# Top-k attention and an MLP mixer on one core: where the dummy values lie, how many thresholds are negated, and what lengths the planner counts with

## The chip, the cores and the metric

One NeuronCore of a Trainium2 chip runs the whole kernel in one launch. The metric is the device time in microseconds (us) of that core. Engines are named as the profile names them: PE is TensorE's matmul (PEld its weight load), DVE is VectorE, ACT is ScalarE, POOL is GpSimd, SP is SyncE, which here only issues DMAs.

## The reference

For each of 8 batches and 8 heads, with 576 rows of 64 numbers, it computes top-k attention, and then an MLP mixer over the concatenated heads:

```
scores = scale * q @ k.T                       # 576 x 576 for each head
kth    = the 32nd largest of each row          # top_k = 32
attn   = softmax(where(scores >= kth, scores, -1e9))
x      = concat over heads (attn @ v)          # 8 x 576 x 512
h  = relu(x.T @ w_tok1) @ w_tok2;  u = x + h.T
h2 = relu(u @ w_ch1) @ w_ch2;      out = u + h2
```

## The kernel before

The 64 heads are worked in 32 pairs of two. A pair has nine score tiles of 128 rows by 576 columns: four units of two tiles each (one tile for each head) and one unit of one tile, which holds the last 64 rows of both heads. There are 160 units and 288 tiles.

One unit goes through this chain. PE makes the scores into PSUM tiles called big (L363, or L354 for the small unit). ACT copies them to S in SBUF (L417). For each tile DVE takes the top 8 of each of seven segments of the row into cd (L424) and then, with two rounds of MAX8 and MATCH_REPLACE8 and a last MAX8 (L427, L428, L435), an upper threshold thi: an element that is surely in the top 32, at a rank of about 24. ACT takes Sign of S against thi (L438) into sg and sums it into cnt, which tells how many elements lie above thi. POOL multiplies S by sg into X (L441), so that the elements already counted are turned over and the others stay. Beside the 576 products of a tile, X has twelve more columns: DVE writes dummy values into nine of them (L449), large positive or large negative ones by cnt, so that the eighth largest value of the products and the dummies together is just the 32nd largest of the row. DVE's MAX8 over 587 columns finds it: tlo (L453).

With tlo known, a unit takes one of three forms, chosen by the pair and the unit (`FORMS = ("DRDRD", "ADADA")`, pairs in turn). Form D: ACT makes E = exp(S) (L461), DVE negates the unit's thresholds into nt (L463), and POOL makes Z = (S + nt) * 16, clamps it to a mask M and multiplies E by M into Pm (L466, L469, L472). Form R: ACT makes a penalty M (L479), PE makes the scores again and adds the penalty (L500), and ACT takes exp into Pm (L505). Form A: ACT takes exp into a PSUM tile (L510), and DVE compares and multiplies into Pm (L513). A DMA transposes Pm into PT; when the five units of a pair are there, PE multiplies PT by the values (L386) and DVE divides (L401, L402). After every fourth pair the mixer of that batch runs on PE and ACT (L552 to L626), in between the next pairs' work.

No order of this is written out by hand. Each step is added to a planner with an engine, an expected length, a due time and its dependences (`plan.add("DVE", 0.1, due, ...)`). The planner plays the engines forward: on each engine it takes the step that can start first, and among steps that can start at the same moment (within 0.03) the one that is due first. The due times are multiples of T, the planned time for a tile, from the table W. A step on another engine is taken to see a result HOP after its end. Buffers are taken by the planner too: six S, two X, two sg, three Pm, four big. The instructions are then issued in the planned order, and each engine works through its own in that order; the waits between engines are set from what each instruction reads and writes.

The product is written by one instruction for a whole unit. In a unit of two tiles its output is two rows of 576, 588 apart, and the twelve columns of the first tile lie between the two rows:

```
XW = S + 12
out=X.t[:, 0:n, 0:S]                  # L442, the product of n tiles
out=X.t[:, h, S:XW]...[:, :, 0:3]     # L450, the dummy values of tile h
out=nt.t[:, 0:n]                      # L464, the negated thresholds of n tiles
```

The planner lets the dummy values depend on the tile's own Sign alone (`[cts[h]]`, L452). In the built program, the first L449 of a unit waits for POOL, and so for the product.

Of the kernel before, what the change touches and what calls it, by code (L numbers as in the profile page):

```python
# [8 lines left out]
P = 128  # L9
# [5 lines left out]
LOW = float(2.0**20)  # L15
# [11 lines left out]
BIG = float(2.0**60)  # L27
# [18 lines left out]
class Plan:  # L46
# [3 lines left out]
    HOP = 0.07  # L50
# [120 lines left out]
def kernel(  # L171
# [11 lines left out]
    nc = tc.nc  # L183
    f32 = mybir.dt.float32
# [3 lines left out]
    ALU = mybir.AluOpType  # L188
# [20 lines left out]
    def sbt(name, shape, dt):  # L209
        return sb.tile(shape, dt, name=name, tag=name)  # L210
# [22 lines left out]
    tlo = sbt("tlo", [P, NT + 7], f32)  # L233
# [41 lines left out]
    for t in Xs:  # L275
        nc.vector.memset(t[:, :, S:XW], -BIG)
# [14 lines left out]
    def pair_ops(p):  # L291
# [115 lines left out]
        nm = plan.add("DVE", 0.95, tv + T, norm, [o], acq=[rd], use=[O, X])  # L407
# [4 lines left out]
    def unit_ops(i0, n, s, S_, om, p, g, scores, qkT):  # L412
# [28 lines left out]
        xm = plan.add("POOL", 0.06 + 1.22 * n, te + W["xm"] * T, lambda: nc.gpsimd.tensor_tensor(  # L441
            out=X.t[:, 0:n, 0:S], in0=S_.t[:, 0:n, :], in1=sg.t[:, 0:n, :], op=ALU.mult),  # L442
# [16 lines left out]
        if form == "D":  # L459
            E, M, Z, nt = Buf("E"), Buf("M"), Buf("Z"), Buf("nt")  # L460
            ex = plan.add("ACT", 0.14 + 0.43 * n, te + W["ex"] * T, lambda: nc.scalar.activation(  # L461
                out=E.t[:, 0:n, :], in_=S_.t[:, 0:n, :], func=AF.Exp, scale=scale / UP), evs, acq=[E], use=[S_])
# [9 lines left out]
            last = [plan.add("POOL", 0.06 + 1.22 * n, te + W["pm"] * T, lambda: nc.gpsimd.tensor_tensor(  # L472
                out=Pm.t[:, 0:n, 0:S], in0=E.t[:, 0:n, :], in1=M.t[:, 0:n, :], op=ALU.mult),
                [mk, ex], acq=[Pm], use=[E, M])]
        elif form in ("R", "Q"):
# [7 lines left out]
            else:  # L483
                nt, Z = Buf("nt"), Buf("Z")
                tn = plan.add("DVE", 0.08, te + W["tn"] * T, lambda: nc.vector.tensor_scalar(
                    out=nt.t[:, 0:n], in0=tlo[:, r0 - n + 1 : r0 + 1], scalar1=-(1.0 - 2.0**-24), scalar2=None,
                    op0=ALU.mult), ms, acq=[nt])
                zs = [plan.add("POOL", 0.76, te + W["z"] * T + 0.01 * h, lambda h=h: nc.gpsimd.tensor_scalar(
# [3 lines left out]
                ws = [plan.add("POOL", 0.06 + 0.55 * n, te + W["mk"] * T, lambda: nc.gpsimd.tensor_scalar(  # L492
# [378 lines left out]
```

## Time and profile before

| | us |
|---|---|
| median of 3 runs | 1008.28 (1005.54 to 1013.48) |
| the profiled execution | 1007.34 |
| its span, from the first to the last instruction | 1005.5 |
| mean granted clock of TensorE over the span | 0.839 of full speed |
| busy in the span: PE, DVE, ACT, POOL | 840.6, 830.2, 758.1, 707.6 |

The durations that the rows below give come from the profiled execution. Busy time of an engine is the union of its instructions' times; neighbouring instructions on DVE overlap, so the sum over groups is larger than the engine's busy time. A row of a group gives busy time in us and the mean of one instruction in ns, then the idle time of the engine just before these instructions and what ended it. Most of the work runs evenly from about 20 us to 940 us; the last 35 us are the last batch's mixer on PE and ACT.

### The profile page before, as it was taken

Reading aid. Unit: us, or ns where it says so; the run is one execution under the profiler, and the core shown is the slowest. Engines: PE = TensorE matmul, PEld = TensorE weight load, DVE = VectorE, ACT = ScalarE, POOL = GpSimd, SP = SyncE. Lnnn points to the kernel's source line nnn. Section 1 sums busy time; section 2 is a strip of 40 time slices with the busy share of each in tenths; the row PEclk is TensorE's granted clock in tenths of the full one; section 3 lists DMA queues with packets and bytes.
Section 4 is the critical chain, followed back from the end, with each engine's and each line's share of the span. In section 5 each row is a group of like instructions: output and inputs, shape, how many; then the busy total and the mean of one; then the engine's idle time right before and its main releaser. Section 6 shows DMA issues by size and latency. Waiting matters only on the chain.

```text
span 1005.5 us, 19071 instructions
## 1 busy us (share of the span) xinstructions
PE 840.6 (84%) x5318; PEld 475.5 (47%) x5318; DVE 830.2 (83%) x4868; ACT 758.1 (75%) x1415; POOL 707.6 (70%) x478
## 2 busy tenths in 40 slices
PE   6767679897888979989789978789889897889776
PEld 3434445454454544545445544445445454454443
DVE  4888888888888998889898967999988899988820
ACT  5776768887698877889788776888878797888531
POOL 2878876786786778678776767778777787777600
PEclk9575669996699977899599975999879896899878
DMA  6595724346243553535354452445626364332311
GB/s 134 92 166 97 138 61 83 78 88 143 49 93 70 121 117 52 107 70 139 64 93 95 87 112 45 90 95 98 126 55 98 65 142 82 61 58 60 78 30 51
DMA packets 313011, 90.04 MB, mean 90 GB/s; under 512 B 305728, under 2 KB 307648, under 8 KB 312896
## 3 DMA queue, kind: packets, MB, share of 16 engines
q1 hardware_dynamic: 308944, 84.68, 42.2%
q0 software_dynamic: 2752, 3.77, 2.6%
q8 instruction: 43, 0.70, 0.3%
q14 instruction: 72, 0.59, 0.2%
q10 hardware_dynamic: 1200, 0.30, 0.1%
HBM read 35.85 MB, written 9.44 MB: 45 GB/s over the span
## 4 chain that ended last, share of the span: by engine, by line
POOL 34%; DVE 26%; PE 25%; ACT 8%; issue 4%; DMA 2%; SPq 0%; POOLq 0%; ACTq 0%; DVEq 0%
POOL X L441 14%; POOL Pm L472 9%; DVE cd L424 8%; DVE tlo L453 6%; POOL Z L466 6%; PE big L386 6%; PE big L363 5%; PE big L613 5%; PE big L595 5%; POOL M L469 4%; ACT sg L438 3%; DVE cd L428 3%; DVE X L449 2%; DVE nt L463 2%; DVE Pm L513 1%
## 5 line engine op out<-in xcount | busy, mean ns | idle before, releaser
L441 POOL TENSOR_TENSOR X<-S,sg 128x1152 f32<-128x1152 f32 (+1 forms) x160 | 344.1, 2156 | 146.4 <-ACT sg L438 141.2
L424 DVE MAX8 cd<-S 128x8 f32<-128x82 f32 (+1 forms) x2016 | 398.8, 230 | 12.9 <-ACT S L417 12.4
L363 PE MATMUL big<-kT,qT 64*128 64x64 f32 (+1 forms) x1296 | 300.3, 524 | 61.5 <-DVE Pm L513 16.5
L438 ACT ACTIVATE sg<-S,thi 128x576 bf16<-128x576 f32 x288 | 223.1, 775 | 120.6 <-DVE thi L435 112.1
L363 PEld LDWEIGHTS big<-kT,qT 64*128 64x128 f32 x1296 | 160.7, 223 | 199.5 <-issue 90.7
L453 DVE MAX8 tlo<-X 128x8 f32<-128x587 f32 x288 | 219.1, 761 | 0.1
L417 ACT COPY S<-big 128x576 f32<-128x576 f32 x288 | 171.8, 635 | 34.1 <-PE big L363 29.6
L472 POOL TENSOR_TENSOR Pm<-E,M 128x1152 bf16<-128x1152 bf16 (+1 forms) x79 | 169.4, 2145 | 7.0 <-DMA PT<-Pm 0.6
L386 PE MATMUL big<-vb,PT 128*128 128x65 bf16 (+1 forms) x1600 | 138.0, 216 | 34.9 <-DMA PT<-Pm 28.4
L466 POOL TENSOR_SCALAR Z<-S,nt 128x576 f32<-128x576 f32 x142 | 105.7, 745 | 83.6 <-DVE nt L463 71.0
L386 PEld LDWEIGHTS <-PT 128*128 128x128 bf16 (+1 forms) x1600 | 97.2, 106 | 76.6 <-DMA PT<-Pm 30.1
L595 PE MATMUL big<-UT,wc1b 128*128 128x512 bf16 (+1 forms) x768 | 110.7, 299 | 16.3 <-ACT S L417 5.7
L449 DVE TENSOR_SCALAR X<-kdum,cnt 128x9 f32<-128x9 f32 x288 | 53.2, 211 | 84.2 <-POOL X L441 82.5
L613 PE MATMUL big<-wc2b,H 128*128 128x512 bf16 (+1 forms) x480 | 114.8, 383 | 3.1 <-ACT S L417 1.9
L427 DVE MAX8 m<-cd 128x8 f32<-128x14 f32 x576 | 97.2, 170 | 0.1
L428 DVE MATCH_REPLACE8 cd<-m,cd 128x14 f32<-128x14 f32 x576 | 97.2, 169 | 0.0
L595 PEld LDWEIGHTS <-wc1b 128*128 128x128 bf16 x768 | 55.3, 101 | 70.6 <-issue 26.5
L469 POOL TENSOR_SCALAR M<-Z 128x1152 bf16<-128x1152 f32 (+1 forms) x79 | 82.9, 1049 | 6.6
L461 ACT ACTIVATE E<-S 128x1152 bf16<-128x1152 f32 (+1 forms) x79 | 84.2, 1066 | 1.8
L513 DVE SCALAR_TENSOR_TENSOR Pm<-S,tlo,big 128x576 bf16<-128x576 f32 x78 | 62.5, 804 | 10.6 <-ACT big L510 9.8
L601 ACT ACTIVATE H<-big 128x576 bf16<-128x576 f32 x96 | 59.5, 648 | 14.2 <-PE big L595 13.9
L613 PEld LDWEIGHTS <-H 128*128 128x128 bf16 (+1 forms) x480 | 44.5, 101 | 50.0 <-issue 4.8
(74 smaller groups left out, 852.0 us busy)
## 6 DMA issues: line engine op xcount, KB each, us to landing
qL<-in_q_dram SPq DMA_DIRECT2D x64, 128.0 KB, 2.8
vL<-in_v_dram SPq DMA_DIRECT2D x64, 128.0 KB, 2.8
out_dram<-ob SPq DMA_DIRECT2D x16, 512.0 KB, 3.3
kL<-in_k_dram SPq DMA_DIRECT2D x62, 128.0 KB, 2.8
PT<-Pm SPq DMA_TRANSPOSE x160, 3.4
wc1b<-in_moe_w_ch_dram POOLq DMA_DIRECT2D x4, 384.0 KB, 5.2
wc2b<-in_moe_w_ch_dram POOLq DMA_DIRECT2D x4, 384.0 KB, 5.4
qL<-in_q_dram SPq DMA_DIRECT2D x64, 16.0 KB, 2.3
```

The source lines that it names most:

```text
L363: nc.tensor.matmul(out=flat(bs[h].t)[:, lo:hi], lhsT=qT.t[r, g * P : (g + 1) * P], rhs=kT.t[r, lo:hi], start=True, stop=stop,)
L386: nc.tensor.matmul(out=o[:, g, :], lhsT=src[0:kr, (5 * h if g < 4 else 0) + j, :], rhs=vb.t[0:kr, j, h, :], start=(j == 0), stop=(j == 4),)
L417: evs = [plan.add("ACT", 0.54, t + W["ev"] * T + W["evh"] * h * T, lambda h=h: nc.scalar.copy(out=S_.t[:, h, :], in_=flat(s[h].t)[:, 0:S]) ...
L424: segs = [plan.add("DVE", 0.146, th + W["seg"] * T + 0.01 * a, lambda a=a, cd=cd, h=h: nc.vector.max(cd.t[:, a, :], S_.t[:, h, bounds[a] : ...
L428: c_ = lambda n_, cd=cd, m8=m8: (lambda: nc.vector.match_replace(cd.t[:, :, 0:n_], m8.t[:, :], cd.t[:, :, 0:n_], NEG))
L438: cts.append(plan.add("ACT", 0.77, th + W["ct"] * T, lambda h=h, i=i, r=r: nc.scalar.activation(out=sg.t[:, h, :], in_=S_.t[:, h, :], func ...
L441: xm = plan.add("POOL", 0.06 + 1.22 * n, te + W["xm"] * T, lambda: nc.gpsimd.tensor_tensor(out=X.t[:, 0:n, 0:S], in0=S_.t[:, 0:n, :], in1= ...
L453: m = plan.add("DVE", 0.69, te + W["m5"] * T + 0.3 * h * T, lambda h=h, r=r: nc.vector.max(tlo[:, r : r + 8], X.t[:, h, 0 : XW - 1]), [dm, ...
L466: zs = [plan.add("POOL", 0.76, te + W["z"] * T + 0.01 * h, lambda h=h: nc.gpsimd.tensor_scalar(out=Z.t[:, h, :], in0=S_.t[:, h, :], scalar ...
L472: last = [plan.add("POOL", 0.06 + 1.22 * n, te + W["pm"] * T, lambda: nc.gpsimd.tensor_tensor(out=Pm.t[:, 0:n, 0:S], in0=E.t[:, 0:n, :], i ...
L595: nc.tensor.matmul(out=flat(pb.t)[:, lo:hi], lhsT=wc1b[:, cc, fc * P : (fc + 1) * P], rhs=UT.t[:, cc, lo:hi], start=(cc == 0), stop=(cc == ...
L613: nc.tensor.matmul(out=pb.t[0:r, h, 0:C], lhsT=H2.t[:, fc, cs], rhs=wc2b[:, fc, :], start=(fc == 0), stop=False)
```

## The change

Three things are changed. First, X becomes one flat row of 2 x 588 columns: twelve columns for the first tile's dummies, the two tiles' products in one run of 1152, twelve columns for the second tile's dummies. A tile's MAX8 reads 588 columns, its own products and its own dummies. The dummies of both tiles now lie outside of what the product writes. Secondly, a unit of two tiles negates three thresholds instead of two (the third belongs to an earlier tile and is not used); nt and tlo become one column wider. Thirdly, the planner's lengths, HOP and most due times get other numbers; nothing else in the planner is changed.

```diff
 W = dict(
-    T=2.9, ev=1.3, evh=0.95, seg=0.55, t2=1.2, ct=2.4, xm=2.8, dm=3.0, m5=3.6, ex=3.45, tn=3.4,
+    T=2.85, ev=1.35, evh=1.0, seg=0.55, t2=1.2, ct=3.2, xm=2.8, dm=3.1, m5=3.6, ex=3.45, tn=3.4,
...
-    HOP = 0.07
+    HOP = 0.15
...
-    slots("nt", 3, [P, 2], f32)
+    slots("nt", 3, [P, 3], f32)
...
-    Xs = slots("X", 2, [P, 2, XW], f32)
+
+    Xs = slots("X", 2, [P, 2 * XW], f32)
...
+    nc.vector.memset(tlo[:, NT + 7 : NT + 8], 0.0)
...
-        nc.vector.memset(t[:, :, S:XW], -BIG)
+        nc.vector.memset(t[:, 0 : XW - S], -BIG)
+        nc.vector.memset(t[:, XW + S : 2 * XW], -BIG)
...
-        xm = plan.add("POOL", 0.06 + 1.22 * n, te + W["xm"] * T, lambda: nc.gpsimd.tensor_tensor(
-            out=X.t[:, 0:n, 0:S], in0=S_.t[:, 0:n, :], in1=sg.t[:, 0:n, :], op=ALU.mult),
+        xm = plan.add("POOL", 0.12 + 1.11 * n, te + W["xm"] * T, lambda: nc.gpsimd.tensor_tensor(
+            out=X.t[:, XW - S : XW - S + n * S].rearrange("p (h c) -> p h c", h=n), in0=S_.t[:, 0:n, :], in1=sg.t[:, 0:n, :], op=ALU.mult),
...
-            dm = plan.add("DVE", 0.1, te + W["dm"] * T, lambda h=h, i=i: nc.vector.tensor_scalar(
-                out=X.t[:, h, S:XW].rearrange("p (a b) -> p a b", a=3)[:, :, 0:3],
+            dm = plan.add("DVE", 0.125, te + W["dm"] * T, lambda h=h, i=i: nc.vector.tensor_scalar(
+                out=X.t[:, h * (XW + S) : h * (XW + S) + XW - S].rearrange("p (a b) -> p a b", a=3)[:, :, 0:3],
...
-                tlo[:, r : r + 8], X.t[:, h, 0 : XW - 1]), [dm, xm, order_t2[1]], use=[X])
+                tlo[:, r : r + 8], X.t[:, h * XW : (h + 1) * XW]), [dm, xm, order_t2[1]], use=[X])
...
-                out=nt.t[:, 0:n], in0=tlo[:, r0 - n + 1 : r0 + 1], scalar1=-(1.0 - 2.0**-24), scalar2=None,
+                out=nt.t[:, 0 : 2 * n - 1], in0=tlo[:, r0 - n + 1 : r0 + n], scalar1=-(1.0 - 2.0**-24), scalar2=None,
```

Of the other due times, these move: z 4.3 to 5.1, rw 4.5 to 3.7, eg 5.3 to 4.9, ea 3.6 to 2.8, st 4.55 to 4.05, pv 6.0 to 4.8, mlp 13.05 to 11.85. A dozen planned lengths move by up to a fifth, such as 0.76 to 0.835 for Z.

How the order moves is shown at two places. In these rows cd, m, X, tlo, nt, S and sg are the tiles named above with their buffer numbers, and a bracket names the engines that an instruction waits for. Lines after the change are three higher than before (L452 is L449 of before, L456 is L453, L427 is L424, L430 is L427, L431 is L428, L438 is L435, L441 is L438, L420 is L417, L464 is L461).

The first place is DVE, at the first unit of pair 12. Before, its dummies (L449) stand here:

```order
L428 MATCH_REPLACE cd2_96<-m83_101,cd2_96 128x7x2 [waits DVE_49]
L424 MAX cd0_94<-S5_90 128x8
L427 MAX m83_101<-cd2_96 128x8 [waits DVE_49]
L449 TENSOR_SCALAR X0_109<-kdum_63,cnt_69 128x3x3 [waits Pool_49]
L449 TENSOR_SCALAR X0_109<-kdum_63,cnt_69 128x3x3
L428 MATCH_REPLACE cd2_96<-m83_101,cd2_96 128x7x5 [waits DVE_49]
L424 MAX cd0_94<-S5_90 128x8
L435 MAX thi_70<-cd2_96 128x8 [waits DVE_49]
```

After the change the dummies of the same unit stand at the same place, without a wait:

```order
L431 MATCH_REPLACE cd2_96<-m83_101,cd2_96 128x7x2 [waits DVE_49]
L427 MAX cd3_97<-S3_88 128x8
L430 MAX m83_101<-cd2_96 128x8 [waits DVE_49]
L427 MAX cd3_97<-S3_88 128x8
L431 MATCH_REPLACE cd2_96<-m83_101,cd2_96 128x7x5 [waits DVE_49]
L452 TENSOR_SCALAR X0_109<-kdum_63,cnt_69 128x3x3 x2
L438 MAX thi_70<-cd2_96 128x8 [waits DVE_49]
```

Twelve rows further on, DVE comes to that unit's MAX8 over X, which now carries the wait for POOL:

```order
L438 MAX thi_70<-cd3_97 128x8 [waits DVE_49]
L427 MAX cd0_94<-S3_88 128x8 x2
L452 TENSOR_SCALAR X1_110<-kdum_63,cnt_69 128x3x3 [waits Activation_49]
L456 MAX tlo_71<-X0_109 128x8 [waits Pool_49]
L452 TENSOR_SCALAR X1_110<-kdum_63,cnt_69 128x3x3 [waits Activation_49]
L456 MAX tlo_71<-X0_109 128x8 [waits DVE_49]
```

At that place before, the MAX8 over X stands as far behind the dummies, and waits for nothing more:

```order
L435 MAX thi_70<-cd0_94 128x8 [waits DVE_49]
L424 MAX cd3_97<-S5_90 128x8
L453 MAX tlo_71<-X0_109 128x8
L424 MAX cd3_97<-S5_90 128x8
L453 MAX tlo_71<-X0_109 128x8 [waits DVE_49]
L449 TENSOR_SCALAR X1_110<-kdum_63,cnt_69 128x3x3 [waits Pool_49]
```

So the wait for the product moves from the dummies to the MAX8 that reads them; next to it stand the next unit's dummies, which now wait for ACT's Sign.

The second place is ACT, at the second unit of the same pair, whose two Signs (L438) have other work between them. Before:

```order
L438 ACTIVATE sg1_108,cnt_69<-S3_88,thi_70 128x576 [waits DVE_49,Activation_49]
L417 COPY S4_89<-big0_135 128x576 [waits PE_49,Activation_49]
L417 COPY S4_89<-big2_137 128x576 [waits PE_49]
L461 ACTIVATE E2_93<-S5_90 128x1152 [waits Activation_49,Pool_49]
L438 ACTIVATE sg1_108,cnt_69<-S3_88,thi_70 128x576 [waits DVE_49]
```

After the change, with the same unit in S1 in place of S3:

```order
L441 ACTIVATE sg1_108,cnt_69<-S1_86,thi_70 128x576 [waits DVE_49,Activation_49]
L420 COPY S0_85<-big0_135 128x576 [waits PE_49,Activation_49]
L420 COPY S0_85<-big2_137 128x576 [waits PE_49]
L441 ACTIVATE sg1_108,cnt_69<-S1_86,thi_70 128x576 [waits DVE_49]
L464 ACTIVATE E0_91<-S3_88 128x1152 [waits Activation_49,Pool_49]
```

The exponential of a D unit moves behind the second Sign. POOL's order hardly moves: nearly everywhere it is two products, two Z, one M and one Pm, before and after.

## Rows read from the trace of the kernel before

**Rows 1.** The page's first part: busy us, share of the span, instructions
```profile
PE 840.6 (84%) x5318; PEld 475.5 (47%) x5318; DVE 830.2 (83%) x4868; ACT 758.1 (75%) x1415; POOL 707.6 (70%) x478
```

**Rows 2.** Who waited for whom, whole span: total us, times, longest us
```profile
POOL X L441 <- ACT sg L438: 141.2, 54, 16.6
...
DVE X L449 <- POOL X L441: 82.5, 61, 3.1
POOL Z L466 <- DVE nt L463: 71.0, 50, 4.6
...
PE big L386 <- DMA PT<-Pm: 28.4, 14, 4.3
...
DVE cd L424 <- ACT S L417: 12.4, 6, 8.5
```

**Rows 3.** The page's chain that ended last: shares of the span by line
```profile
POOL X L441 14%; POOL Pm L472 9%; DVE cd L424 8%; DVE tlo L453 6%; POOL Z L466 6%; PE big L386 6%; PE big L363 5%; PE big L613 5%; PE big L595 5%; POOL M L469 4%; ACT sg L438 3%; DVE cd L428 3%; DVE X L449 2%; DVE nt L463 2%; DVE Pm L513 1%
```

**Rows 4.** Stretches of 100 us: busy of PE, PEld, DVE, ACT, POOL; clock, DMA
```profile
20.00:120.00 100.00, 70.57 (x331) 42.63 (x330) 87.38 (x539) 74.56 (x142) 81.24 (x62) 0.65 0.71 123
...
320.00:420.00 100.00, 88.39 (x580) 50.46 (x581) 90.94 (x529) 80.27 (x150) 79.16 (x52) 0.86 0.47 95
...
620.00:720.00 100.00, 87.51 (x600) 49.89 (x601) 92.06 (x533) 84.58 (x159) 77.70 (x52) 0.97 0.47 92
...
sum 900.00, PE 762.11 PEld 432.41 DVE 785.83 ACT 711.06 POOL 678.14; mean PE 84.68 PEld 48.05 DVE 87.31 ACT 79.01 POOL 75.35
```

**Rows 5.** Groups by form: busy us, mean ns of one, idle before, releasers
```profile
L424 DVE MAX8 cd<-S 128x8 f32<-128x82 f32 x1440 | 308.5, 230 | 12.9 <-ACT S L417 12.4 <-issue 0.2
L441 POOL TENSOR_TENSOR X<-S,sg 128x1152 f32<-128x1152 f32 x128 | 303.8, 2375 | 122.9 <-ACT sg L438 117.6 <-DVE cd L428 3.8 <-DVE m L427 0.9
...
L438 ACT ACTIVATE sg<-S,thi 128x576 bf16<-128x576 f32 x288 | 223.1, 775 | 120.6 <-DVE thi L435 112.1 <-POOL Z L466 5.8 <-POOL M L469 2.1
L453 DVE MAX8 tlo<-X 128x8 f32<-128x587 f32 x288 | 219.1, 761 | 0.1
L417 ACT COPY S<-big 128x576 f32<-128x576 f32 x288 | 171.8, 635 | 34.1 <-PE big L363 29.6 <-DVE cd L428 2.1 <-PE big L354 1.6
...
L438 ACT ACTIVATION_READ_ACCUMULATOR sg<-S,thi 128x1 f32 x288 | 55.3, 192 | 0.0
...
L449 DVE TENSOR_SCALAR X<-kdum,cnt 128x9 f32<-128x9 f32 x288 | 53.2, 211 | 84.2 <-POOL X L441 82.5 <-ACT sg L438 1.3
...
L463 DVE TENSOR_SCALAR nt<-tlo 128x2 f32<-128x2 f32 x63 | 28.5, 453 | 0.0
...
L463 DVE TENSOR_SCALAR nt<-tlo 128x1 f32<-128x1 f32 x16 | 2.3, 143 | 0.0
```

**Rows 6.** DVE's timeline, 371 to 380 us: start, us, instruction, idle before it
```profile
372.88 0.18 DVE L427 MAX8 m<-cd 128x8 f32<-128x35 f32 x1
375.36 0.35 DVE L449 TENSOR_SCALAR X<-kdum,cnt 128x9 f32<-128x9 f32 x2 [2.30 <-POOL X L441]
...
377.96 0.75 DVE L453 MAX8 tlo<-X 128x8 f32<-128x587 f32 x1
```

**Rows 7.** POOL's timeline, 366 to 386 us
```profile
372.95 2.37 POOL L441 TENSOR_TENSOR X<-S,sg 128x1152 f32<-128x1152 f32 x1
377.12 2.37 POOL L441 TENSOR_TENSOR X<-S,sg 128x1152 f32<-128x1152 f32 x1 [1.80 <-ACT sg L438]
```

**Rows 8.** L449 and the writers of nt: ns min/median/max, first and last start, forms
```profile
L449 DVE TENSOR_SCALAR X<-kdum,cnt x288: 194/212/223, 20.3 to 950.5; 128x9 f32<-128x9 f32 x144
...
L463 DVE TENSOR_SCALAR nt<-tlo x79: 129/167/1806, 24.4 to 940.2; 128x2 f32<-128x2 f32 x63, 128x1 f32<-128x1 f32 x16
```

**Rows 9.** DVE's timeline, 353 to 357 us
```profile
354.21 1.71 DVE L463 TENSOR_SCALAR nt<-tlo 128x2 f32<-128x2 f32 x1
```

**Rows 10.** POOL's timeline, 338 to 362 us
```profile
353.53 2.37 POOL L441 TENSOR_TENSOR X<-S,sg 128x1152 f32<-128x1152 f32 x1 [3.89 <-ACT sg L438]
356.02 1.56 POOL L466 TENSOR_SCALAR Z<-S,nt 128x576 f32<-128x576 f32 x2
```

More of the change, by code (lines that the diff above doesn't have):

```diff
@@ L405, in norm @@
             )
-        nm = plan.add("DVE", 0.95, tv + T, norm, [o], acq=[rd], use=[O, X])
+        nm = plan.add("DVE", 0.86, tv + T, norm, [o], acq=[rd], use=[O, X])
         mixed.setdefault(b, []).append(nm)
@@ L416, in unit_ops @@
         te = t + (n - 1) * T
-        evs = [plan.add("ACT", 0.54, t + W["ev"] * T + W["evh"] * h * T, lambda h=h: nc.scalar.copy(
+        evs = [plan.add("ACT", 0.525, t + W["ev"] * T + W["evh"] * h * T, lambda h=h: nc.scalar.copy(
             out=S_.t[:, h, :], in_=flat(s[h].t)[:, 0:S]), [om], use=[s[h], S_]) for h in range(n)]
@@ L491, in unit_ops @@
                     use=[S_, nt, Z]) for h in range(n)]
[L492 removed]
+                ws = [plan.add("POOL", 0.27 + 0.48 * n, te + W["mk"] * T, lambda: nc.gpsimd.tensor_scalar(
                     out=Wm.t[:, 0:n, :], in0=Z.t[:, 0:n, :], scalar1=0.0, scalar2=-float(2.0**40), op0=ALU.min,
@@ L504, in unit_ops @@
             og = plan.add("PE", 1.05 + 0.25 * n, te + W["og"] * T, again, ws, acq=es, use=[Wm] + qkT)
-            last = [plan.add("ACT", 0.56, te + W["eg"] * T + 0.2 * h, lambda h=h: nc.scalar.activation(
+            last = [plan.add("ACT", 0.535, te + W["eg"] * T + 0.2 * h, lambda h=h: nc.scalar.activation(
                 out=Pm.t[:, h, 0:S], in_=flat(es[h].t)[:, 0:S], func=AF.Exp, scale=scale / UP),
@@ L509, in unit_ops @@
             Ep = [Buf("big") for _ in range(n)]
-            ex = [plan.add("ACT", 0.57, te + W["ea"] * T + 0.2 * h, lambda h=h: nc.scalar.activation(
+            ex = [plan.add("ACT", 0.58, te + W["ea"] * T + 0.2 * h, lambda h=h: nc.scalar.activation(
                 out=flat(Ep[h].t)[:, 0:S], in_=S_.t[:, h, :], func=AF.Exp, scale=scale / UP),
                 [xm], acq=[Ep[h]], use=[S_]) for h in range(n)]
-            last = [plan.add("DVE", 0.75, te + W["st"] * T + 0.01 * h, lambda h=h: nc.vector.scalar_tensor_tensor(
+            last = [plan.add("DVE", 0.72, te + W["st"] * T + 0.01 * h, lambda h=h: nc.vector.scalar_tensor_tensor(
                 out=Pm.t[:, h, 0:S], in0=S_.t[:, h, :], scalar=tlo[:, r0 - h : r0 - h + 1],
@@ L585, in mlp_ops @@
                 o = plan.add("PE", 1.2, d, f, [h1, l2], acq=[pb] + ([UT] if cc == 0 else []), use=[X, H1, UT])
-                uts.append(plan.add("ACT", 0.57, d + 1, lambda cc=cc, pb=pb: nc.scalar.copy(
+                uts.append(plan.add("ACT", 0.525, d + 1, lambda cc=cc, pb=pb: nc.scalar.copy(
                     out=UT.t[:, cc, :], in_=flat(pb.t)[:, 0:S]), [o], use=[pb, UT]))
@@ L600, in mlp_ops @@
             o = plan.add("PE", 1.05, d, f, uts + l3, acq=[pb] + ([H2] if fc == 0 else []), use=[UT, H2])
-            h2.append(plan.add("ACT", 0.58, d + 1, lambda fc=fc, pb=pb: nc.scalar.activation(
+            h2.append(plan.add("ACT", 0.535, d + 1, lambda fc=fc, pb=pb: nc.scalar.activation(
                 out=H2.t[:, fc, :], in_=flat(pb.t)[:, 0:S], func=AF.Relu), [o], use=[pb, H2]))
@@ L625, in mlp_ops @@
                     dep = [o]
-            e = plan.add("ACT", 0.13 + 0.43 * sn, d + 1, lambda pb=pb, ob=ob, r=r, sn=sn: nc.scalar.copy(
+            e = plan.add("ACT", 0.1 + 0.4 * sn, d + 1, lambda pb=pb, ob=ob, r=r, sn=sn: nc.scalar.copy(
                 out=ob.t[0:r, 0:sn, :], in_=pb.t[0:r, 0:sn, 0:C]), [o], use=[pb, ob])
```

34 lines of the change are left out of this document (17 added, 17 removed).

## The prediction

> **What bounds the kernel now.** I read the busy shares first. No engine is full: PE 84%, DVE 83%, ACT 75%, POOL 70% of the span [rows 1]. Four engines that near to each other, none full, mean that waits between them set the pace, so the next view is who waited for whom. There the long entries form one loop: POOL's product waits 141.2 us for ACT's Sign, the Sign waits 112.1 us for DVE's thi [rows 5], and DVE waits 82.5 us in 61 places for the product to end. The first and third of these are [rows 2]. The chain that ended last runs over the same loop: POOL's product alone has 14% of the span [rows 3], which is 141 us, or some sixty products of 2.375 us [rows 5]; as many as DVE waits for.
>
> The groups by form tell where DVE stands while it waits. The 82.5 us lie in front of L449, which writes the dummies. In front of L453, which reads product and dummies, there is 0.1 us [rows 5]. The timeline shows one such wait: DVE ends a MAX8 at 373.06, stands idle for 2.30 us and goes on with L449 at 375.36 [rows 6]; the product of that unit ran on POOL from 372.95 to 375.32 [rows 7]. The tile's MAX8 over X comes only at 377.96 [rows 6], after 2.25 us of segment and threshold work for other tiles. That work didn't need the product, and stood in the queue behind an instruction that doesn't need it either.
>
> DVE has a second loss that is booked as busy time. Negating two thresholds takes 453 ns in the mean, one threshold 143 [rows 5]; the longest took 1806 [rows 8]. The one at 354.21 ends at 355.92 [rows 9], just after the product that POOL ran from 353.53 to 355.90 [rows 10]. Over 63 instructions this is 28.5 us less 63 x 0.143 = 9.0, so 19.5 us.
>
> **The change part by part.** *The dummies' place.* Product and dummies no longer overlap, so L449 waits only for its own Sign, and the wait for the product stands at the MAX8. In the new order, between the dummies of the unit shown and its MAX8 (twelve rows, of which the two ends are shown) stand ten segment MAX8, two rounds of MAX8 and MATCH_REPLACE8, two thi and one more dummy. In the timeline before, a like piece took 2.25 us (from the dummies' end at 375.71 to 377.96) [rows 6]. The mean wait was 82.5 / 61 = 1.35 us, the longest 3.1 [rows 2]. So nearly each of the 61 waits is shorter than the work that now stands in front of it; I take 2.5 us off for the few that are longer, and 80 us of DVE's waiting is gone at first order.
>
> What is late next decides how much of the 80 us reaches the end, and no row shows a run without these waits, so I bound it. If all of it does, the gain is 80. The other end comes from the best 100 us that each other engine had in this trace. PE did 762.1 us of work in 900 us, and its best share was 88.39%; at that share throughout, the 900 us shrink to 762.1 / 0.8839 = 862, a gain of 38. For ACT it is 711.1 / 0.8458 = 841, a gain of 59, and for POOL 678.1 / 0.8124 = 835, a gain of 65 [rows 4]. These shares aren't hard limits, since the best stretches hold waits of this kind too; below 38 it goes only if a wait of a new kind appears (rivals). I take 50, between PE's 38 and ACT's 59, because these two are nearest to being full. What is late then is PE, in its queue's order, above all the 28.4 us in which it waits for transposed Pm [rows 2].
>
> L449 can now wait for ACT in its own right. Sign and its sum take 0.775 + 0.192 = 0.97 us [rows 5]; ACT's queue can put two copies of 0.635 in between, which makes 2.2. In the new order nearly all dummies stand more than 2 us of DVE work behind their own thi. I cost this at 0; without that cover it is at most the 2.2 us for each dummy that stands right behind its thi.
>
> *Three thresholds.* If the wait for POOL goes, up to 19.5 us of DVE time comes free; if it stays, nothing does. The rows don't settle it. L449, which reads nine numbers, never took over 223 ns in 288 times [rows 8], though POOL was mostly busy; but it differs from L463 in two more ways, a scalar read from memory and an output laid in three rows of three against an input in one row. The instruction with three thresholds is like that with two in all but the count. I go by this nearer row and take 0; the other end stays as a rival.
>
> [...]
>
> *The rest.* The MAX8 reads 588 columns instead of 587: by 230 ns at 82 and 761 at 587 [rows 5] that is 1 ns, 0.3 us over 288. Writing the product as one run instead of two costs nothing: its time goes by the 1152 products, 2375 ns [rows 5]. Three more small memsets stand at the head, where DVE waits up to 8.5 us for the first scores [rows 2]. They cost 0.
>
> *Due times and lengths.* No instruction is added; what stands before what changes. The places read in the order go the right way, if at all: POOL's sequence is the same, and at the place shown on ACT an exponential no longer stands between two Signs. In front of the values' matmuls on PE stand as many score units as before, or one fewer. I cost this at 0, bounded on the good side by the case in which all 80 us arrive, on the bad side by the last rival.
>
> The sum: the span of 1005.5 less 50 is 955.5. Around the span lie 1007.34 - 1005.5 = 1.8 us, which makes 957.3 for a run like the profiled one; the median was 0.9 above it. I predict 958 us.
>
> **The rivals.** First, the odd count does free the negation. DVE then gains 19.5 us more; at the rate of the first part (50 of 80) some 12 arrive, and it is 946 us. For it speaks L449's 223 ns, against it the likeness of three to two.
>
> Second, all 80 us arrive, since DVE paces the loop and the others follow: 958 - 30 = 928 us. For it: DVE's share was up to 92.06%, and in the same stretch the granted clock was 0.97 and PE passed 600 matmuls, against 580 at a clock of 0.86 and 331 at 0.65 [rows 4], so PE can do more when it is fed. Against it: with 785.8 us of work in 820, DVE would be at 96%.
>
> Third, the wait only moves. DVE gets to the MAX8 sooner, but so do the Signs that it feeds, and POOL's products then queue behind Z, M and Pm; DVE then waits at the MAX8 as long as it did at the dummies, with at most 5 us won: about 1003 us. For it: POOL's best share of 81% was in the stretch with the lowest clock and the worst progress [rows 4]. Against it: POOL itself stood idle for 141.2 us waiting for Sign [rows 2], so it has room.
>
> Fourth, slower: the new due times (Sign at 3.2 T instead of 2.4) put Signs behind ACT's copies. The place is ACT's queue, the price 0.635 us for each unit whose last Sign has one more copy in front [rows 5]. With all 160 units this is 102 us against the 50 won: 1060 us. It decides from 80 units on, where it eats the 50; at the place shown the opposite happens.
>
> **How the numbers follow.** The forecast has a chance of 0.46, with a range of its own from 938 to 980 (ACT's and PE's bounds, with some 10 us on either side); the odd count that helps 0.20; all arriving 0.13; the wait that only moves 0.12; slower 0.09. The first three are faster by over 1%, which is about what a measurement of this kernel can tell from no change (10 us): 0.79. The third rival counts as within 1%, 0.12, and the last as slower, 0.09. The range reaches down to 916, where all 80 us and the 12 of the negation arrive, and up to the 1003 of the wait that moves; what lies outside is the slower case and some of the fringe.
>
> **What would show it.** Right: in front of the line that writes the dummies the idle time falls from 84 us to under 10; in front of the MAX8 over X there is a wait for POOL of 5 to 30 us in place of 0.1; the 141 us that POOL waits for Sign shrink by some 30; PE's share rises over 88%. The negation of three thresholds still shows single durations over 1.5 us and a mean over 300 ns, or, if the first rival holds, at most 200 ns. Wrong: a wait at the MAX8 of 60 us or more (third rival), Sign standing ready while ACT copies, with POOL's wait for it over 180 us (fourth), or a new long wait on PE that no row here names.

## The result, and the profile after

The changed kernel takes 938.86 us (median of 4 runs, 936.03 to 945.99) where the kernel before, beside it, took 1010.75 (4 runs): a ratio of 0.9305, with a 95% interval from 0.9236 to 0.9374. The forecast was 958 us, with a range of 916 to 1003. The profiled executions have spans of 938.2 and 1005.5 us, so 67.3 us went there.

The page's first part and the chain that ended last, of the changed kernel, answer to [rows 1, 3]:

```profile
PE 799.9 (85%) x5260; PEld 461.3 (49%) x5318; DVE 834.4 (89%) x4871; ACT 754.2 (80%) x1415; POOL 708.4 (76%) x478
...
DVE 38%; PE 38%; ACT 13%; POOL 4%; issue 4%; DMA 3%; SPq 0%; DVEq 0%; ACTq 0%; POOLq 0%
DVE cd L427 13%; PE big L366 9%; PE big L616 9%; PE big L389 9%; DVE tlo L456 8%; DVE cd L431 4%; ACT sg L441 3%; DVE Pm L516 3%; PE big L598 3%; ACT S L420 3%; DMA PT<-Pm 2%; DVE m L430 2%; PE big L336 2%; DVE nt L466 2%; ACT E L464 2%
```

POOL's product (L444 now) headed the chain with 14% and has left the list; POOL as a whole has 4%. DVE and PE share the chain evenly. DVE's busy time hardly moved (830.2 to 834.4), so it does nearly the same work in a shorter time; 11 us more of it are the negation (28.5 to 39.7, below).

The groups by form of the changed kernel answer to [rows 5] (busy us, mean ns, idle before, releasers):

```profile
L427 DVE MAX8 cd<-S 128x8 f32<-128x82 f32 x1440 | 313.4, 229 | 11.4 <-ACT S L420 11.1
L444 POOL TENSOR_TENSOR X<-S,sg 128x1152 f32<-128x1152 f32 x128 | 303.9, 2379 | 86.4 <-ACT sg L441 81.5 <-PE big L503 4.4
L366 PE MATMUL big<-kT,qT 64*128 64x512 f32 x648 | 249.8, 748 | 36.5 <-DVE Pm L516 15.3 <-ACT S L420 11.7 <-DVE Xb L405 3.7
L441 ACT ACTIVATE sg<-S,thi 128x576 bf16<-128x576 f32 x288 | 224.1, 779 | 56.0 <-DVE thi L438 50.0 <-POOL Z L469 3.6 <-POOL X L444 0.8
L456 DVE MAX8 tlo<-X 128x8 f32<-128x588 f32 x288 | 218.8, 760 | 2.7 <-POOL X L444 2.5
...
L452 DVE TENSOR_SCALAR X<-kdum,cnt 128x9 f32<-128x9 f32 x288 | 52.4, 207 | 9.1 <-ACT sg L441 9.1
...
L466 DVE TENSOR_SCALAR nt<-tlo 128x3 f32<-128x3 f32 x63 | 39.7, 630 | 0.0
```

In front of the dummies (L452) the idle time fell from 84.2 us to 9.1, all of it for ACT's Sign. In front of the MAX8 over X (L456) only 2.7 us appeared. And the negation of three thresholds (L466) is no cheaper: 630 ns in the mean, against 453 for two before.

Of the waits of the changed kernel (total us, times, longest), these two are used below:

```profile
POOL X L444 <- ACT sg L441: 107.4, 51, 15.4
...
PE big L389 <- DMA PT<-Pm: 32.9, 12, 5.9
```

The unit that stood for 2.30 us in [rows 6] meets the same situation again. DVE's timeline of the changed kernel, at the first unit of pair 12:

```profile
351.90 0.35 DVE L452 TENSOR_SCALAR X<-kdum,cnt 128x9 f32<-128x9 f32 x2
352.16 0.22 DVE L438 MAX8 thi<-cd 128x8 f32<-128x56 f32 x1
...
354.04 0.38 DVE L427 MAX8 cd<-S 128x8 f32<-128x83 f32 x2
354.33 0.21 DVE L452 TENSOR_SCALAR X<-kdum,cnt 128x9 f32<-128x9 f32 x1
354.45 0.78 DVE L456 MAX8 tlo<-X 128x8 f32<-128x588 f32 x1
```

and POOL's:

```profile
351.85 4.71 POOL L444 TENSOR_TENSOR X<-S,sg 128x1152 f32<-128x1152 f32 x2
```

Two products run back to back from 351.85, at about 2.36 us each, the first until about 354.2. As before, DVE reaches the dummies just when the product begins. Now it writes them at once, does its other work, and comes to the MAX8 at 354.45, when the product has just ended.

### The profile page after: what moved, and what is told of

It reads as the page before. It is cut to its first block, busy times and chain, and to the rows that moved or that the text cites. A ratio compares the mean times of both kernels' runs of the same rounds, so it can differ in the third digit from the quotient of the medians.

```text
span 938.2 us, 19036 instructions
## 1 busy us (share of the span) xinstructions
PE 799.9 (85%) x5260; PEld 461.3 (49%) x5318; DVE 834.4 (89%) x4871; ACT 754.2 (80%) x1415; POOL 708.4 (76%) x478
## 4 chain that ended last, share of the span: by engine, by line
DVE 38%; PE 38%; ACT 13%; POOL 4%; issue 4%; DMA 3%; SPq 0%; DVEq 0%; ACTq 0%; POOLq 0%
DVE cd L427 13%; PE big L366 9%; PE big L616 9%; PE big L389 9%; DVE tlo L456 8%; DVE cd L431 4%; ACT sg L441 3%; DVE Pm L516 3%; PE big L598 3%; ACT S L420 3%; DMA PT<-Pm 2%; DVE m L430 2%; PE big L336 2%; DVE nt L466 2%; ACT E L464 2%
## 5 line engine op out<-in xcount | busy, mean ns | idle before, releaser
L444 POOL TENSOR_TENSOR X<-S,sg 128x1152 f32<-128x1152 f32 (+1 forms) x160 | 344.2, 2160 | 112.3 <-ACT sg L441 107.4
L427 DVE MAX8 cd<-S 128x8 f32<-128x82 f32 (+1 forms) x2016 | 404.1, 229 | 11.4 <-ACT S L420 11.1
L366 PE MATMUL big<-kT,qT 64*128 64x64 f32 (+1 forms) x1296 | 276.2, 510 | 36.5 <-DVE Pm L516 15.3
L441 ACT ACTIVATE sg<-S,thi 128x576 bf16<-128x576 f32 x288 | 224.1, 779 | 56.0 <-DVE thi L438 50.0
L366 PEld LDWEIGHTS big<-kT,qT 64*128 64x128 f32 x1296 | 150.0, 217 | 161.5 <-issue 91.1
L456 DVE MAX8 tlo<-X 128x8 f32<-128x588 f32 x288 | 218.8, 760 | 2.7 <-POOL X L444 2.5
L420 ACT COPY S<-big 128x576 f32<-128x576 f32 x288 | 173.7, 639 | 30.9 <-PE big L366 29.4
L389 PE MATMUL big<-vb,PT 128*128 128x65 bf16 (+1 forms) x1600 | 134.3, 213 | 40.4 <-DMA PT<-Pm 32.9
L598 PE MATMUL big<-UT,wc1b 128*128 128x64 bf16 (+1 forms) x745 | 105.4, 287 | 18.8 <-ACT H L604 10.5
L431 DVE MATCH_REPLACE8 cd<-m,cd 128x14 f32<-128x14 f32 (+1 forms) x576 | 96.6, 168 | 0.0
L430 DVE MAX8 m<-cd 128x8 f32<-128x14 f32 (+1 forms) x576 | 96.4, 168 | 0.1
L464 ACT ACTIVATE E<-S 128x1152 bf16<-128x1152 f32 (+1 forms) x79 | 84.7, 1072 | 1.6
L452 DVE TENSOR_SCALAR X<-kdum,cnt 128x9 f32<-128x9 f32 x288 | 52.4, 207 | 9.1 <-ACT sg L441 9.1
```

Of the source, the lines that this page charges most:

```text
L366: nc.tensor.matmul(out=flat(bs[h].t)[:, lo:hi], lhsT=qT.t[r, g * P : (g + 1) * P], rhs=kT.t[r, lo:hi], start=True, stop=stop,)
L389: nc.tensor.matmul(out=o[:, g, :], lhsT=src[0:kr, (5 * h if g < 4 else 0) + j, :], rhs=vb.t[0:kr, j, h, :], start=(j == 0), stop=(j == 4),)
L420: evs = [plan.add("ACT", 0.525, t + W["ev"] * T + W["evh"] * h * T, lambda h=h: nc.scalar.copy(out=S_.t[:, h, :], in_=flat(s[h].t)[:, 0:S] ...
L427: segs = [plan.add("DVE", 0.146, th + W["seg"] * T + 0.01 * a, lambda a=a, cd=cd, h=h: nc.vector.max(cd.t[:, a, :], S_.t[:, h, bounds[a] : ...
L430: m_ = lambda n_, cd=cd, m8=m8: (lambda: nc.vector.max(m8.t[:, :], cd.t[:, :, 0:n_]))
L431: c_ = lambda n_, cd=cd, m8=m8: (lambda: nc.vector.match_replace(cd.t[:, :, 0:n_], m8.t[:, :], cd.t[:, :, 0:n_], NEG))
```

## The experiments

All ratios are to the kernel before, timed beside each run on the same chip.

**Undoing the parts.** The change has three. The first run does the place of X alone, the second the numbers alone.

```diff
 # e1_place_only: the kernel before, with
-    Xs = slots("X", 2, [P, 2, XW], f32)
+    Xs = slots("X", 2, [P, 2 * XW], f32)
...
 # e2_numbers_only: the changed kernel, with
-    Xs = slots("X", 2, [P, 2 * XW], f32)
+    Xs = slots("X", 2, [P, 2, XW], f32)
-                out=nt.t[:, 0 : 2 * n - 1], in0=tlo[:, r0 - n + 1 : r0 + n],
+                out=nt.t[:, 0:n], in0=tlo[:, r0 - n + 1 : r0 + 1],
...
```

> The kernel before with X laid out flat and nothing else: the planner's numbers, and so the order, stay those of before, and two thresholds are negated. If the false wait at the dummies is the cause, this alone gives most of the 72 us: a ratio to before of 0.93 to 0.95, with under 10 us of idle time before the dummies. If the new due times are the cause, the ratio stays over 0.98.

> The changed kernel with the old layout of X and two thresholds: only the planner's lengths, HOP and due times are new. If the place of the dummies is the cause, the ratio to before is 0.985 to 1.015 and DVE again waits 70 to 90 us for POOL before the dummies. If the due times are the cause, it is 0.93 to 0.96.

The place alone: 956.06 us, ratio 0.9451 (0.9405 to 0.9497). The numbers alone: 1025.63 us, ratio 1.0144 (1.0095 to 1.0193). Both the ratio and the idle time below are those expected if the false wait is the cause. So the place of the dummies is the main cause, and the numbers without the new place make the kernel slower by 1.4%. The place also makes the product one run instead of two, but that is worth nothing by itself: the product takes 2378 ns there and took 2375 before. The groups by form of the place alone, where the lines are one higher than before:

```profile
L454 DVE MAX8 tlo<-X 128x8 f32<-128x588 f32 x288 | 219.6, 763 | 2.1 <-POOL X L442 1.9
...
L450 DVE TENSOR_SCALAR X<-kdum,cnt 128x9 f32<-128x9 f32 x288 | 52.4, 208 | 4.0 <-ACT sg L439 4.0
L464 DVE TENSOR_SCALAR nt<-tlo 128x2 f32<-128x2 f32 x63 | 46.4, 737 | 0.0
```

Before dummies and MAX8 DVE stands idle for 6.1 us in place of 84.3; the negation, though, grew from 453 to 737 ns, and its longest from 1806 to 2145. Who waited for whom, in the run with the numbers alone (total us, times, longest):

```profile
POOL X L443 <- ACT sg L440: 155.6, 61, 15.3
ACT sg L440 <- DVE thi L437: 124.9, 103, 3.7
DVE X L451 <- POOL X L443: 100.2, 75, 2.3
```

The false wait grew from 82.5 us to 100.2 [rows 2]. The planner doesn't know of it, so numbers that are nearer to the truth elsewhere needn't place the dummies any better; that is a reading, and no run tries it further. The second expectation had that wait at 70 to 90 us, so it missed; its ratio lies just inside what was expected for a neutral result (1.0144 in a window up to 1.015), but with an interval clear of 1.

The two alone add up to a ratio of about 0.945 x 1.014 = 0.959. Both together, without the odd count, make 0.926 (next run). So the numbers are worth about 2% on the new layout and cost 1.4% on the old one.

**Two thresholds or three.** The changed kernel with the old count:

```diff
 # e3_two_thresholds
-                out=nt.t[:, 0 : 2 * n - 1], in0=tlo[:, r0 - n + 1 : r0 + n],
+                out=nt.t[:, 0:n], in0=tlo[:, r0 - n + 1 : r0 + 1],
```

> The changed kernel with two thresholds negated instead of three. If the odd count does nothing, the time is that of the changed kernel within 0.5% (ratio to before 0.925 to 0.936) and the mean of the negation stays near 630 ns. If the odd count helps in part, it is slower by 5 us or more and the mean rises above 750 ns.

It took 936.64 us, ratio 0.926 (0.9215 to 0.9305): the changed kernel's time. The group of L466 with two thresholds:

```profile
L466 DVE TENSOR_SCALAR nt<-tlo 128x2 f32<-128x2 f32 x63 | 39.4, 626 | 0.0
```

626 ns against 630, and a longest of 2384 against 2403: the odd count does nothing.

**What does free the negation.** The dummies' instruction never waited inside its duration (at most 223 ns in 288 times [rows 8]), and it reads nine numbers in one row and writes three rows of three. So the negation got that shape (nt 12 columns wide, tlo 8 wider still, the seven or eight surplus values unused):

```diff
 # e4_nine_to_rows
-                out=nt.t[:, 0 : 2 * n - 1], in0=tlo[:, r0 - n + 1 : r0 + n], scalar1=-(1.0 - 2.0**-24),
+                out=nt.t[:, :].rearrange("p (a b) -> p a b", a=3)[:, :, 0:3],
+                in0=tlo[:, r0 - n + 1 : r0 - n + 10].rearrange("p (a b) -> p a b", a=3), scalar1=-(1.0 - 2.0**-24),
```

> The changed kernel with the negation reading nine columns in one row and writing three rows of three, the shape of the dummies. If unequal odd dimensions of source and output are what keeps an instruction from waiting for POOL, the negation falls from 630 ns to about 210 with no duration over 250, some 26 us of DVE time come free, and the ratio to before falls from 0.93 to 0.905 to 0.92. If the wait comes from something else (the scalar operand, or the place in the order), its mean stays near 630 and the time stays.

928.37 us, ratio 0.9184 (0.9138 to 0.923). The writers of nt (ns min/median/max), in the changed kernel and then in this run:

```profile
L466 DVE TENSOR_SCALAR nt<-tlo x79: 140/160/2403, 20.9 to 871.1; 128x3 f32<-128x3 f32 x63, 128x1 f32<-128x1 f32 x16
```

```profile
L466 DVE TENSOR_SCALAR nt<-tlo x79: 142/153/166, 22.1 to 861.9; 128x9 f32<-128x9 f32 x79
```

and, in this run, their group by form (busy us, mean ns):

```profile
L466 DVE TENSOR_SCALAR nt<-tlo 128x9 f32<-128x9 f32 x79 | 12.0, 152 | 0.0
```

No instruction takes over 166 ns, where single ones took up to 2403 in the changed kernel. The scalar is an immediate in both, so it isn't the scalar from memory that keeps the dummies' instruction from waiting. The count (nine) and the three rows came together here; no run has nine numbers in one row on both sides, so the runs don't say which of the two is needed, nor whether unequal odd dimensions, as the expectation has it, are the reason. The pages' first parts, of e3_two_thresholds and of this run:

```profile
PE 803.0 (86%) x5318; PEld 460.9 (49%) x5318; DVE 833.8 (89%) x4871; ACT 753.8 (81%) x1415; POOL 708.3 (76%) x478
```

```profile
PE 798.0 (86%) x5318; PEld 457.5 (49%) x5318; DVE 807.1 (87%) x4871; ACT 752.0 (81%) x1415; POOL 707.6 (76%) x478
```

DVE's busy time falls from the changed kernel's 834.4 to 807.1, by 27.3 us; the span falls by 938.2 - 926.5 = 11.7. Against e3_two_thresholds, timed beside it, DVE's busy time falls by 26.7 and the span by 935.4 - 926.5 = 8.9.

**Which of the numbers.** Three runs take the numbers apart, on the new layout. The first has the new lengths and HOP with the old table of due times, the second the new due times with the old lengths and HOP, the third the place and HOP alone.

```diff
 # e5_lengths_only: the changed kernel, with
-    T=2.85, ev=1.35, evh=1.0, seg=0.55, t2=1.2, ct=3.2, xm=2.8, dm=3.1, m5=3.6, ex=3.45, tn=3.4,
+    T=2.9, ev=1.3, evh=0.95, seg=0.55, t2=1.2, ct=2.4, xm=2.8, dm=3.0, m5=3.6, ex=3.45, tn=3.4,
...
 # e6_dues_only: the changed kernel, with
-    HOP = 0.15
+    HOP = 0.07
...
-        zs = [plan.add("POOL", 0.835, te + W["z"] * T + 0.01 * h,
+        zs = [plan.add("POOL", 0.76, te + W["z"] * T + 0.01 * h,
...
 # e12_place_and_hop: e1_place_only, with
-    HOP = 0.07
+    HOP = 0.15
```

> The changed kernel with the due times of before and the new planned lengths and HOP. With the place alone the ratio was 0.945, with everything 0.93. If the lengths and HOP bring the rest, the ratio is 0.925 to 0.935; if the due times do, it stays at 0.94 to 0.95.

> The changed kernel with the new due times and the planned lengths and HOP of before. If the due times bring what the place alone does not, the ratio is 0.925 to 0.935; if the lengths and HOP do, it stays at 0.94 to 0.955.

> The kernel before with X laid out flat and HOP at 0.15 in place of 0.07, all other numbers as before. The place alone gave 0.945, place with lengths and HOP 0.928. If HOP is the part of the numbers that helps, the ratio is 0.925 to 0.936; if the lengths are, it stays at 0.94 to 0.95.

| run | place | lengths | HOP | due times | ratio (95%) |
|---|---|---|---|---|---|
| e1_place_only | new | old | old | old | 0.9451 (0.9405 to 0.9497) |
| e12_place_and_hop | new | old | new | old | 0.9415 (0.9366 to 0.9464) |
| e6_dues_only | new | old | old | new | 0.9387 (0.9349 to 0.9424) |
| e5_lengths_only | new | new | new | old | 0.9284 (0.924 to 0.9328) |
| e3_two_thresholds | new | new | new | new | 0.926 (0.9215 to 0.9305) |

The expectations of e5 and e12 came out on the side of the lengths; e6 lies in neither of its two windows. HOP alone can't be told from nothing. With the lengths and HOP new, the due times can't be told from nothing either (0.9284 and 0.926). Between e12 and e5, which differ in the lengths (and in the count of thresholds, which does nothing), the intervals don't meet: the new lengths are what brings the rest, about 1.4%. Some twenty of them move, the dummies' by a quarter: planned at 0.1 before and 0.125 now, where two of them take from 351.90 to 352.16 in the timeline above, 0.13 us each. The new due times with the old lengths and HOP lie between, below the place alone, with intervals that overlap.

**What sets the time now.** Two engines share the chain, so each got a little more to do, without a change in any value.

```diff
 # e7_dve_more: each tile's dummies written twice
-            dm = plan.add("DVE", 0.125, te + W["dm"] * T, lambda h=h, i=i: nc.vector.tensor_scalar(
+            dm = plan.add("DVE", 0.125, te + W["dm"] * T, lambda h=h, i=i: [nc.vector.tensor_scalar(
...
-                scalar1=cnt[:, i : i + 1], scalar2=-BIG, op0=ALU.add, op1=ALU.mult), [cts[h]], use=[X])
+                scalar1=cnt[:, i : i + 1], scalar2=-BIG, op0=ALU.add, op1=ALU.mult) for _ in range(2)],
...
 # e8_pe_more: the last 64 columns of a two-tile unit's scores made four times; e10_pe_less_more: twice (1 for 3)
-            for lo, hi in ((0, SM), (SM, S)):
+            for lo, hi in ((0, SM), (SM, S)) + ((SM, S),) * (3 if stop else 0):
                 for h in range(2):
```

> The changed kernel in which DVE writes each tile's dummies twice, 288 more instructions at about 0.125 us apart, 36 us of DVE work that changes no value. If DVE paces the loop now, 25 to 40 us of it reach the end (ratio to before 0.955 to 0.97). If PE, ACT and POOL bound it, as the forecast had it, under 18 us do (ratio below 0.948).

> The changed kernel in which PE makes the last 64 columns of the scores of each two-tile unit four times instead of once, 384 more pairs of small matmuls at about 0.1 us a pair, some 25 to 40 us of PE work that changes no value. If PE's share bounds the time, as the forecast had it, most of it reaches the end (over 20 us, ratio over 0.95). If DVE paces the loop, under 12 us do (ratio below 0.942).

> The changed kernel in which PE makes the last 64 columns of the scores of each two-tile unit twice, a third of the PE work that was added with four times: by that run some 32 us of PE busy time. If PE is as near to setting the time as DVE, 16 to 30 us reach the end (ratio 0.947 to 0.96). If a small addition still finds room in PE's waits, under 12 us do (ratio below 0.943).

| run | median us | ratio (95%) | busy added | span added | share that arrived |
|---|---|---|---|---|---|
| e7_dve_more | 983.6 | 0.9729 (0.9688 to 0.977) | DVE 54.7 | 44.8 | 82% |
| e8_pe_more | 1003.19 | 0.992 (0.9876 to 0.9964) | PE 95.7 | 60.6 | 63% |
| e10_pe_less_more | 951.81 | 0.9393 (0.9346 to 0.9439) | PE 25.6 | 10.7 | 42% |

The busy times are those of the page's first part, less those of the changed kernel (834.4 and 799.9); the spans are 983.0, 998.8 and 948.9, less 938.2. The pages' first parts of the three runs:

```profile
PE 820.2 (83%) x5260; PEld 471.0 (48%) x5318; DVE 889.1 (90%) x5159; ACT 761.2 (77%) x1415; POOL 708.5 (72%) x478
```

```profile
PE 895.6 (90%) x6785; PEld 566.5 (57%) x6854; DVE 834.8 (84%) x4871; ACT 757.3 (76%) x1415; POOL 708.9 (71%) x478
```

```profile
PE 825.5 (87%) x5830; PEld 494.4 (52%) x5830; DVE 835.7 (88%) x4871; ACT 755.6 (80%) x1415; POOL 708.5 (75%) x478
```

The first two additions by far missed the size that was expected, so the shares count here and not the ratios: by busy time a second writing of the dummies cost DVE 54.7 / 288 = 0.19 us instead of 0.125, and a repeated pair of small matmuls cost PE 95.7 / 384 = 0.25 us instead of 0.1. That the ratios of the first two lie over the line set for "paced by" is owed to that in part. The third came out as expected if a small addition still finds room in PE's waits (10.7 us, under 12). The shares are rough, above all that of the third: 58 of 5318 matmuls are missing from the changed kernel's profile, and against e3_two_thresholds, which has them all, e10 adds 22.5 us of PE work of which 13.5, or 60%, arrive.

Their chains, DVE's addition first, then PE's larger one:

```profile
DVE 71%; PE 15%; ACT 7%; issue 3%; DMA 2%; POOL 1%; SPq 0%; DVEq 0%; ACTq 0%; POOLq 0%
```

```profile
PE 57%; DVE 20%; ACT 10%; POOL 5%; issue 4%; DMA 3%; SPq 0%; DVEq 0%; ACTq 0%; POOLq 0%
```

More work on DVE makes DVE 71% of the chain; more on PE makes PE 57%. Neither engine paced the changed kernel alone: of what is added to either, a good part arrives. That the two are just even isn't shown. Adding to DVE costs 82% of what is added; taking 27.3 us from it (e4_nine_to_rows) gave only 11.7 / 27.3 = 43%, or 33% against e3_two_thresholds. In that run's chain PE has 41% and DVE 26%, so PE holds more of the end there:

```profile
PE 41%; DVE 26%; ACT 15%; POOL 9%; DMA 4%; issue 4%; SPq 0%; DVEq 0%; POOLq 0%; ACTq 0%
```

**Towards a better version.** With the negation free, DVE waited 43.0 us in front of the division for the values' matmuls (L404, 31.7 in the changed kernel). Two runs try it with other due times.

```diff
 # e9_nine_pv_late: e4_nine_to_rows, with
-    z=5.1, mk=4.9, pm=4.55, rw=3.7, og=4.8, eg=4.9, ea=2.8, st=4.05, tr=3.4, pv=4.8, fin=9.4,
+    z=5.1, mk=4.9, pm=4.55, rw=3.7, og=4.8, eg=4.9, ea=2.8, st=4.05, tr=3.4, pv=6.0, fin=9.4,
 # e11_nine_old_dues: e4_nine_to_rows, with the whole table W of the kernel before
```

> The kernel whose negation reads nine columns and writes three rows of three (0.918), with the values' matmuls due at 6.0 T as before the change instead of 4.8 T. There DVE waited 43 us in front of the division for these matmuls, 11 us more than in the changed kernel. If their early due time is why only 10 of 28 us arrived, that wait falls under 35 us and the ratio goes to 0.905 to 0.913; if not, it stays at 0.913 to 0.923.

> The kernel with the negation of nine columns, with the due times of before and the new lengths and HOP. If the due times do nothing, the ratio is 0.91 to 0.923, as with the new due times. If the old ones with freed negation are better or worse, it lies below 0.908 or above 0.925.

e9_nine_pv_late took 924.8 us, ratio 0.9115 (0.9069 to 0.9161), and e11_nine_old_dues 928.12 us, ratio 0.9161 (0.9107 to 0.9214), which is what was expected if the due times do nothing. The waits before the division in the first of them:

```profile
DVE rd L404 <- PE big L389: 41.5, 24, 8.4
```

The wait didn't go, so that guess was wrong; the ratio lies inside what was expected for a yes, but its interval overlaps that of e4_nine_to_rows, and the two profiled spans are even (926.0 and 926.5). All three versions with the free negation beat the kernel before clearly, and their intervals end below the changed kernel's (0.923, 0.9161 and 0.9214 against its lower end of 0.9236), though the first only just. That the free negation helps is clearest between e3_two_thresholds and e4_nine_to_rows, which were timed together: 936.33 to 937.18 us against 927.64 to 930.45. Between the three nothing is shown.

## Why the prediction was right, and where it was off

*What bounds the kernel.* Right. The loop over POOL's product and the dummies was the pace; with that wait gone the product left the chain, as the page above shows. What is late next was half right: I named PE, above all its wait for transposed Pm, which is 32.9 us now; but the chain gives DVE and PE 38% each.

*The dummies' place.* The first-order sum was 80 us of DVE's waiting gone, with 50 of them arriving. The place alone took DVE's idle time before dummies and MAX8 from 84.3 us to 6.1, and the span from 1005.5 to 954.3, by 51.2: the term was right to the size. But something lies inside it that the prediction didn't have. The negation's wait grew at the same time, from 28.5 us busy to 46.4, and its mean from 453 to 737 ns. Of 79 negations 19 took over 250 ns before and 36 in the changed kernel; all of these ran beside a product and ended 0.01 to 0.03 us after it. I read the growth as DVE reaching the negation more often while POOL runs a product. So of the 78 us freed 18 were spent there, and 51 of the remaining 60 arrived. The 50 itself was picked between two bounds of which neither held (next point), so that it met 51 is in part luck. The dummies' own wait for Sign, which I put at 0, came to 9.1 us in the changed kernel.

*The bounds from the other engines' best stretch.* A weak step. PE at its best share of 88.39% was to limit the gain to 38, ACT to 59; the gain was 67. PE's share over the span is 85%, not over 88% as I had looked for, so that sign failed. Two things were wrong with the bound. The best stretch depends on where the trace is cut: one that starts at 260 us in the trace of before had PE at 91.43%, and by it the bound is 762.1 / 0.9143 = 834, a gain of 66.

```profile
260.00:360.00 100.00, 91.43 (x619) 51.37 (x620) 89.45 (x525) 82.42 (x155) 75.77 (x51) 0.91 0.43 90
```

And a share measured amid waits is no ceiling. In the changed kernel PE came to 92.39%, ACT to 88.28% and DVE to 98.88%, which was 92.06% at best in [rows 4]; so the doubt whether DVE could be at 96%, with which I argued against the second rival, didn't hold either:

```profile
420.00:520.00 100.00, 89.13 (x585) 50.57 (x591) 98.88 (x562) 88.28 (x167) 80.80 (x53) 0.88 0.54 108
520.00:620.00 100.00, 92.39 (x627) 53.88 (x633) 96.36 (x576) 87.92 (x167) 83.03 (x56) 0.86 0.53 100
```

Nor is PE's busy time a fixed amount of work: it fell from 840.6 us to 799.9 (803.0 in e3_two_thresholds, with all its matmuls on record). The mean granted clock went from 0.839 to 0.863 of full speed (0.865 in e3_two_thresholds), and the score matmul's mean from 769 ns to 748. Busy time times clock is 840.6 x 0.839 = 705 before and 803.0 x 0.865 = 695 in e3_two_thresholds, so the busy time fell mostly with the clock.

*Three thresholds.* Taken at 0, and 0 it is (e3_two_thresholds): the rival with the odd count is out. The runs show which shapes wait for POOL, but not why: 2 into 2 and 3 into 3 do (626 and 630 ns in the mean), 1 into 1 doesn't (148 ns in the mean in the changed kernel, though all 16 ran beside a product), and 9 into three rows of 3 doesn't (at most 166 ns). The wait itself is seen once more in the changed kernel, DVE's timeline first, then POOL's:

```profile
442.25 2.36 DVE L466 TENSOR_SCALAR nt<-tlo 128x3 f32<-128x3 f32 x1
```

```profile
442.21 2.37 POOL L444 TENSOR_TENSOR X<-S,sg 128x1152 f32<-128x1152 f32 x1 [3.08 <-ACT sg L441]
```

The product runs from 442.21 to 444.58, the negation of three from 442.25 to 444.61: it waited for the whole of it, as in [rows 9, 10].

*Due times and lengths.* This is the term that was mis-sized. "I cost this at 0": it is worth 938.2 - 954.3 = -16 us of span on the new layout, nearly all of the difference between the forecast and the result. I had looked at the order in a few places and found nothing that matters; the runs show that the planned lengths bring it. How they bring it isn't settled. POOL's wait for Sign doesn't tell: it is 114.8 us in e1_place_only and 92.8 in e5_lengths_only, but 107.4 in the changed kernel, which is as fast as e5, and 101.3 in e12_place_and_hop, which is slower. PE's own time says more. The page of e1_place_only, whose granted clock is 0.850:

```profile
PE 821.4 (86%) x5318; PEld 470.3 (49%) x5318; DVE 844.3 (88%) x4870; ACT 754.5 (79%) x1415; POOL 708.5 (74%) x478
```

PE is not busy for 954.3 - 821.4 = 132.9 us there and for 935.4 - 803.0 = 132.4 in e3_two_thresholds, whose clock is 0.865. So PE waits no less in sum: what the numbers save is in its busy time, at a higher clock. Whether the clock is a cause of that or follows from PE being fed in another way, no run tells.

*The rivals.* Nearest in size came the first, the odd count that helps (946 us), but its mechanism is out: two thresholds take the same time as three. That all 80 arrive (928 us) is 11 us off; the place alone didn't do that, it was the lengths that added to it. The wait that only moves is out: 2.7 us before the MAX8, where even the forecast had 5 to 30. The slower case is out: POOL waits 107.4 us for Sign, less by 34, as foreseen.

## What to carry to other kernels

In these programs the waits went by the range that an instruction's output spans: the columns between two rows of the product's output waited for it (82.5 us in 61 waits [rows 2]). Columns beyond that range didn't, even in the same buffer: in the changed kernel all 9.1 us before the dummies are for ACT's Sign, and before the change, too, the dummies of a one-tile unit, which lie behind its only row, were written while the product ran (45.89 us, in a product from 45.34 to 46.62).

```profile
45.34 1.28 POOL L441 TENSOR_TENSOR X<-S,sg 128x576 f32<-128x576 f32 x1
45.89 0.20 DVE L449 TENSOR_SCALAR X<-kdum,cnt 128x9 f32<-128x9 f32 x1
```

Look in the waits for an instruction that is released by a producer whose result it doesn't read, and move its data out of that range. In a queue that is worked in order, the gain is the work that stands behind the needless wait (here 78 us less of DVE's waiting, and 51.2 us of span, in e1_place_only); and a planner that doesn't know of such a wait can get worse when its numbers get better, as the numbers did here on the old layout (ratio 1.0144). Before a remedy for a wait inside an instruction's duration is believed, look at the maximum duration of the instruction in the profile: the mean of 453 ns hid a longest of 1806 and a median of 167 over all the negations [rows 8], and with the odd count they are 2403 and 160.

## What was not expected of the hardware

A VectorE instruction on three numbers took up to 2.4 us in the changed kernel (2403 ns), where another of its shape took 0.15 (at 346.38 us). The wait lies inside its own duration, where no wait is listed (0.0 us of idle time before L466) and the engine counts as busy; the changed kernel's busy time on DVE holds 27 us more (834.4 and 807.1) than that of e4_nine_to_rows, which does the same work. Writing nine numbers into the same nine places a second time took longer than writing another tile's nine, where the timelines show it: two writings to the same places took 0.38 us to the next instruction's start (366.28 to 366.66 in e7_dve_more), and two to the places of two tiles 0.26 (351.90 to 352.16 in the timeline of the changed kernel).

```profile
366.28 0.46 DVE L452 TENSOR_SCALAR X<-kdum,cnt 128x9 f32<-128x9 f32 x2
366.66 0.76 DVE L457 MAX8 tlo<-X 128x8 f32<-128x588 f32 x1
```

And a pair of small fp32 matmuls of 64 columns repeated into the same PSUM columns added 0.25 us to PE's busy time (e8_pe_more), and 25.6 / 128 = 0.20 in e10_pe_less_more.
